# First-batch q in one load per head pair, even tokens above odd ones, and k^T v held in both partition halves

## The chip, the cores and the metric

The kernel runs on one core of one Trainium2 chip. The metric is the device time of one execution in microseconds (us); several executions are timed and their median is told. One further execution is profiled: its instructions, DMA packets and semaphore events are recorded, and "the trace" below means that record.

The core has five engines that run beside one another. TensorE (PE in the profile, with PEld for its weight loads) multiplies matrices from SBUF into PSUM. VectorE (DVE), ScalarE (ACT) and GpSimd (POOL) work on elements. SyncE (SP) here only issues DMA transfers; POOL and ACT issue some as well. They meet through semaphores.

## The reference

```python
# 8 batches, 8 heads, 576 tokens, head_dim 64, all fp32
kv  = einsum('bhsd,bhse->bhde', k, v)            # k^T v, one 64x64 matrix per head, no softmax
out = einsum('bhsd,bhde->bhse', q, kv)           # u = q (k^T v)
out = out / sqrt(mean(out*out, -1) + 1e-6) * g_norm
x   = out.transpose(0, 2, 1, 3).reshape(4608, 512)
gate = sigmoid(x @ w_gate); val = x @ w_val      # 512 -> 1536
return (gate * val) @ w_out                      # 1536 -> 512, float32
```

The three weight matrices arrive as float64 and are converted to fp32 in the kernel.

## The kernel before

**The large part.** The 4608 tokens are worked in 9 chunks of 512 (c = 0 to 8). Chunk 0 uses plain products (lines 666 and 913); the chunks after it use a fast scheme with 26 products instead of 32 or 64 (lines 1037 and 1139), whose sums of operands run on DVE, ACT and POOL beside TensorE. The attention of batch b is worked a stage ahead of the chunks that read it. All of this is behind the change and its instructions are the same before and after, in the same order on TensorE.

**The start, where the change lies.** Before chunk 0 can start, the first batch's eight heads are worked as four pairs, n = 0 to 3, each pair being two neighbouring heads, e = 0 and 1. `load_kv(n)` and `load_q(n)` bring k, v and q of a pair from HBM on SP's queue, in the order k, v, q of pair 0, of pair 1, and so on, with the first unit of weights between. A partition p of the 96 that are used holds six neighbouring tokens, 6p to 6p + 5, of each head (j = 0 to 5). k and v come as one transfer each, in which a partition's piece of one head is a single run of 6 x 64 x 4 = 1536 bytes. q comes as two transfers, one per head, and is laid out as [96, j, e, 64] in SBUF, so each run is 256 bytes.

`attention(n, ...)` returns the steps of a pair, named in the order below by their tokens:

- KV (`kv_mm`, line 346): 12 matmuls of 64 output rows, six tokens j by two heads e. Head e's k^T v lands in PSUM partitions 64e to 64e + 63.
- KVO (`kv_out`, line 350): DVE copies it, [128, 64], to SBUF.
- Q (`q_mm`, line 356): six transposes on TensorE, one per j, of [96, 2 heads x 64] to [128, 96]. So q^T has head 0 in partitions 0 to 63 and head 1 in 64 to 127.
- QO (`q_out`, line 361): ACT copies q^T to SBUF.
- U (`u_mm`, line 373): 20 matmuls of 64 x 64 x 64. The contraction runs over head e's 64 partitions; the result of 64 tokens goes to PSUM partitions r = 0 or 64, alternating, and to PSUM bank e (`ps[:, e]`, 512 fp32 to a bank). The four combinations of the half read (e) and the half written (r) follow one another.
- SQ, SUM, ROOT, NORM (lines 378 to 392): the norm, on ACT and DVE.
- X, XO (lines 400 and 409): five transposes back, and ACT's copies into `xT`, the 512 x tokens operand of the chunks.

The order of everything around these steps is written out by hand in the string `order` (line 699): tokens such as KV0, Q0, KVO0, and between them `warmN` (N matmuls of the identity with itself, whose result nobody reads), `gU.i`/`vU.i` and `agU.i`/`avU.i` (steps of the weights' conversion on DVE and ACT, lines 212 to 254), `bF.i.m` (products of chunk 0, line 666) and `wU` (a load of weights). Each engine runs its own instructions strictly in that order:

```
w1 w2 warm10 KV0 warm4 Q0 KVO0 QO0 warm3 U0 KV1 KVO1 Q1 SQ0 QO1 SUM0 ROOT0 g0.0 warm4 U1 NORM0 SQ1 warm5 X0
SUM1 ag0.0 ROOT1 g0.1 ag0.1 NORM1 XO0 warm1 KV2 Q2 KVO2 QO2 X1 g0.2 XO1 g0.3 warm2 U2 g0.4 v0.0 SQ2 b0.0.0
v0.1 av0.1 SUM2 v0.3 b0.0.1 KV3 ROOT2 av0.0 NORM2 Q3 KVO3 X2 v0.2 w3 g1.0 QO3 U3 XO2 ag1.0 ...
```

In this stage POOL fills the identity and then has nothing to do until it issues the loads of batch 1's q (line 122, from 22 us), which go into memory that the first batch's k, v and q tiles held.

The other attention code, `heads_run` for batches 1 to 7 (line 497), also has 64 x 64 x 64 matmuls, with four combinations of the half read and the half written in turn; its q and k, v come in other layouts, and the change leaves it alone. The tail of k^T v of those batches (line 436) and the rest of it (line 447) are two more kinds of small matmul that are used below: 64 x 64 over two halves read and two halves written, and 128 x 64 over two halves written.

Of the kernel before, what the change touches and what calls it, by code (L numbers as in the profile page):

```python
# [10 lines left out]
FP32 = mybir.dt.float32  # L11
# [10 lines left out]
def kernel(  # L22
# [11 lines left out]
    nc = tc.nc  # L34

    B, H, S, HD = q.shape
    T, DM = out.shape
    DF = moe_w_gate.shape[1]
    P = 128
    NHP = H // 2  # L40
    NJ = 6
    NP = S // NJ
    JH = NJ // 2


    PH = P // 2
    NU = -(-S // P)
# [9 lines left out]
    NRUN = NHP // 2  # L57
    QW = 2 * S

    NK4 = S // P  # L60
    S4 = P * NK4
# [13 lines left out]
    const = ctx.enter_context(tc.tile_pool(name="const", bufs=1))  # L75
# [9 lines left out]
    first = first_ctx.__enter__()  # L85
# [3 lines left out]
    pairs = {n: {} for n in range(B * NHP)}  # L89
# [9 lines left out]

    def load_q(n):  # L100
        h0 = 2 * n
        t = first.tile([NP, NJ, 2, HD], FP32, tag="q", name="q")
        for e in range(2):
            nc.sync.dma_start(out=t[:, :, e, :], in_=q[0, h0 + e].rearrange("(p j) d -> p j d", j=NJ))
        pairs[n]["q"] = t

    q_late = {}
# [190 lines left out]
    for n in range(4):  # L298
        load_kv(n)
        load_q(n)  # L300
        if n in (1, 2):
            load_unit(0, (n - 1,))
# [8 lines left out]
    ident = const.tile([P, P], FP32, name="ident")  # L311


    kvq = const.tile([P, NRUN, 2, HD], FP32, name="kvq")
    kv_ahead = const.tile([P, NRUN, 2, HD], FP32, name="kv_ahead")

    qTs = const.tile([P, QW], FP32, name="qTs")
    sqs = const.tile([P, 2 * NU * P], FP32, name="sqs")
# [13 lines left out]
    def chunk(c):  # L332
        return xT[c]

    def attention(n, at_ps):

        b, m = divmod(n, NHP)
        d = {}
        kv = kvq[:, m // 2, m % 2]

        def kv_mm():
            d["kv"] = ps = at_ps("kv")
            for j in range(NJ):
                js = slice(HD * j, HD * j + HD)
                for e in range(2):
                    nc.tensor.matmul(ps[HD * e:HD * e + HD, 0, 0:HD], pairs[n]["k"][:, e, js], pairs[n]["v"][:, e, js],  # L346
                                     start=(j == 0), stop=(j == NJ - 1))

        def kv_out():
            nc.vector.tensor_copy(out=kv, in_=d["kv"][:, 0, 0:HD])  # L350

        def q_mm():
            d["q"] = ps = at_ps("q")
            for j in range(NJ):
                c0 = NP * (j % JH)
                nc.tensor.transpose(ps[:, j // JH, c0:c0 + NP], pairs[n]["q"][:, j].rearrange("p e d -> p (e d)"),  # L356
                                    ident[0:NP, 0:NP])

        def q_out():
            d["qT"] = qTs[:, S * (n % 2):S * (n % 2) + S]  # L360
            nc.scalar.copy(out=d["qT"].rearrange("p (i n) -> p i n", i=2), in_=d["q"][:, :, 0:JH * NP])  # L361

        def u_mm():


            ps = at_ps("u")
            d["u"] = ps[:, :, 0:NU * HD]
            for i in range(2 * NU):
                t0 = min(PH * i, S - PH)
                r = PH * (i % 2)  # L370
                for e in range(2):
                    es = slice(HD * e, HD * e + HD)
                    nc.tensor.matmul(d["u"][r:r + PH, e, HD * (i // 2):HD * (i // 2) + HD],  # L373
                                     d["qT"][es, t0:t0 + PH], kv[es], start=True, stop=True)

        def u_square():
            d["sq"] = sqs[:, NU * P * (n % 2):NU * P * (n % 2 + 1)].rearrange("p (e c) -> p e c", e=2)
            nc.scalar.activation(out=d["sq"], in_=d["u"], func=AF.Square)

        def u_sum():  # L380
            d["ms"] = sb.tile([P, 2, NU], FP32, tag="ms", name="ms")
            nc.vector.tensor_reduce(out=d["ms"].rearrange("p e i -> p (e i)"),
                                    in_=d["sq"].rearrange("p e (i d) -> p (e i) d", d=HD), axis=AX.X, op=ALU.add)

        def u_root():
            nc.scalar.activation(out=d["ms"], in_=d["ms"], func=AF.Sqrt, bias=eps, scale=1.0 / HD)

        def u_norm():

            nc.vector.reciprocal(d["ms"], d["ms"])  # L390
            d["xn"] = d["sq"].rearrange("p e c -> p (e c)")
            nc.vector.tensor_tensor(out=d["xn"].rearrange("p (i e d) -> p e i d", e=2, d=HD),
                                    in0=d["u"].rearrange("p e (i d) -> p e i d", d=HD),
                                    in1=d["ms"].unsqueeze(3).to_broadcast([P, 2, NU, HD]), op=ALU.mult)

        def x_mm():
            d["x"] = ps = at_ps("x")
            for i in range(NU):
                bank, c0 = divmod(P * i, UX)
                nc.tensor.transpose(ps[:, bank, c0:c0 + P], d["xn"][:, P * i:P * i + P], ident)  # L400

        def x_out():

            s0 = 0
            while s0 < S:
                c, o = divmod(S * b + s0, G)
                i, r = divmod(s0, UX)
                n_ = min(G - o, (UX if i == 0 else S - UX) - r)
                nc.scalar.copy(out=chunk(c)[:, m, o:o + n_], in_=d["x"][:, i, r:r + n_])
                s0 += n_  # L410

        return [kv_mm, kv_out, q_mm, q_out, u_mm, u_square, u_sum, u_root, u_norm, x_mm, x_out]


# [185 lines left out]
    def store(c, t, ot, cols=slice(0, DM), queues=(nc.sync,)):  # L600

        r0 = i = 0
        while r0 < P:
            b, s = divmod(G * c + P * t + r0, S)
            rows = out[S * b:S * b + S, cols]
            if b < NE // NHP:
                j, p = divmod(s, NP)
                n = min(P - r0, NP - p)
                queues[i % len(queues)].dma_start(out=rows.rearrange("(p j) d -> j p d", j=NJ)[j, p:p + n],
                                                  in_=ot[r0:r0 + n, cols])  # L610
            else:

                half, c0 = divmod(s, S // 2)
                n = QB
                queues[i % len(queues)].dma_start(
                    out=rows.rearrange("(p g i) d -> i g p d", p=QB, i=2)[half, c0 // QB],
                    in_=ot[r0:r0 + n, cols])
            r0 += n
            i += 1
# [12 lines left out]
    def mm_ps():  # L632
        return bank((2, 3, 0, 1)[next(turns) % 4])

    def at_ps():
        return psum.tile([P, NAT, 512], FP32, tag="at", name="at")
# [53 lines left out]

    KV, KV_OUT, Q, Q_OUT, U, U_SQUARE, U_SUM, U_ROOT, U_NORM, X, X_OUT = range(11)
    a = [attention(n, early(n)) for n in range(NE)]

    steps = {"KV": KV, "KVO": KV_OUT, "Q": Q, "QO": Q_OUT, "U": U, "SQ": U_SQUARE, "SUM": U_SUM, "ROOT": U_ROOT,
# [13 lines left out]
    for token in order.split():  # L708
        name = token.rstrip("0123456789.")
        n = [int(i) for i in token[len(name):].split(".")]  # L710
# [183 lines left out]
    for some in places.split():  # L894
        p, names = some.split(":")
# [6 lines left out]
    for f in range(2, NFT):  # L902
        if f == NFT - 1:
            last = at_ps()
            ps = last[:, 0], last[:, 1]
        else:
            ps = mm_ps(), mm_ps()
        plain(0, f, ps, {at: at_place.get(2 * NMT * (f - 1) + at, ()) for at in range(2 * NMT)})

    ps = [mm_ps() for _ in range(G // P)]  # L910
# [209 lines left out]
    def second_layer_fast(c, at):  # L1120
# [21 lines left out]
        def finish(i):  # L1142
            _, _, wv, steps = PRODUCTS2[i]
            combine(o, regions, steps, nc.gpsimd)
            give_all(regions, LAST2, i)
            if c > 1 and wv > 7 and wv not in STAY and STREAM.index(wv) + NR < NS:
                load_w((c - 2) * NS + STREAM.index(wv) + NR)
            if c == 1:
                if i in first_loads:
                    load_granule(first_loads[i])  # L1150
            elif i == 16:
                load_granule(NPA * N3 * (c - 1) + NPA - 1)
            if i in dones:
                t = dones[i]
                store(c, t, rows[t], slice(0, DH if c == NG - 1 and t == NT - 1 else DM), ends)
            elif c == NG - 1 and i == 23:
                store(c, NT - 1, rows[NT - 1], slice(DH, DM), ends)
            for step in at.get(next(done), ()):
                step()
            sums_of_h(2)  # L1160
# [38 lines left out]
    for t in range(G // P):  # L1199
        for f in range(NFT - 2, NFT):  # L1200
            second(t, f)
            slot()
        ot = sg_tile()
        nc.scalar.copy(out=ot, in_=ps[t])
        store(0, t, ot)
# [6 lines left out]
    for c in range(1, NG):  # L1212
# [4 lines left out]
        if c + 1 < B:  # L1217
            kv, first_, then = second_batch if c == 1 else feed(c + 1)
# [49 lines left out]
```

## Time and profile before

| | us |
|---|---|
| median of 3 timed executions | 996.3 (996.08 to 996.44) |
| profiled execution | 996.52 |
| its span (first to last instruction of the program) | 994.7 |
| TensorE busy in the span | 989.4 |
| VectorE, ScalarE, GpSimd busy | 715.0, 349.1, 614.1 |
| granted TensorE clock, mean | 1.0 |

The profiled execution spends 1.8 us outside its span. It is 0.2 us longer than the median of the timed ones, so a change of the span in the profile can be added to the median as it is. An fp32 matmul is two records in the trace, a transpose is one. A matmul's record is longer than its share of TensorE's time, since matmuls are pipelined; the time from one record's start to the next one's is what counts for a sum.

### The profile page before, as it was taken

How to read it: one execution, taken by the hardware profiler on the slowest of the kernel's cores; microseconds unless marked ns; L12 is line 12 of the kernel's file. 1: busy time of each engine (PE TensorE's matmuls, PEld its weight loads, DVE VectorE, ACT ScalarE, POOL GpSimd, SP SyncE). 2: the span in 40 equal slices, each digit the busy share in tenths (PEclk: the TensorE clock that was granted, in tenths of full speed). 3: DMA queues.
4: the chain of work that ended last, by engine and by line, in shares of the span. 5: the costliest groups of instructions: out<-in, count | busy, mean ns of one | idle time of the engine just before them, and what ended most of it. 6: DMA issues, size and time to landing. Idle time of an engine off the chain costs nothing.

```text
span 994.7 us, 16605 instructions
## 1 busy us (share of the span) xinstructions
PE 989.4 (99%) x5958; PEld 814.9 (82%) x5958; DVE 715.0 (72%) x1199; ACT 349.1 (35%) x631; POOL 614.1 (62%) x991
## 2 busy tenths in 40 slices
PE   9999999999999999999999999999999999999998
PEld 7454448888888888888888888888888888888887
DVE  5999997898768666785777576866686566756672
ACT  5577523661244213530344124412442133213320
POOL 1349996798169625864386717870786359734963
PEclk9999999999999999999999999999999999999999
DMA  9986507662889568746975677656854455545514
GB/s 275 291 239 219 166 28 210 193 236 89 277 278 282 170 190 275 197 151 195 271 225 162 204 224 248 184 163 210 280 165 156 139 198 190 165 141 172 214 48 123
DMA packets 149523, 194.97 MB, mean 196 GB/s; under 512 B 79840, under 2 KB 121696, under 8 KB 149440
## 3 DMA queue, kind: packets, MB, share of 16 engines
q0 software_dynamic: 22512, 116.41, 35.3%
q1 hardware_dynamic: 120848, 75.66, 26.5%
q10 hardware_dynamic: 6080, 1.84, 0.8%
q8 instruction: 47, 0.77, 0.3%
q14 instruction: 36, 0.29, 0.1%
HBM read 160.04 MB, written 25.56 MB: 187 GB/s over the span
## 4 chain that ended last, share of the span: by engine, by line
PE 99%; ACT 0%; POOL 0%; issue 0%; DVE 0%; POOLq 0%; ACTq 0%
PE mm L1037 54%; PE mm L1139 27%; PE mm L666 7%; PE mm L913 4%; PE at L497 2%; PE mm L727 1%; PE at L447 1%; PE two L666 1%; PE at L666 1%; PE mm L447 1%; PE mm L346 0%; PE two L373 0%; PE two L356 0%; PE at L436 0%; PE two L400 0%; ACT qTs L361 0%
## 5 line engine op out<-in xcount | busy, mean ns | idle before, releaser
L1037 PE MATMUL mm<-xs,w 128*128 128x256 f32 x1428 | 331.3, 379 | 0.0
L1037 PEld LDWEIGHTS mm<-xs,w 128*128 128x128 f32 x1428 | 270.9, 190 | 37.0
L1037 PE MATMUL mm<-xT,w 128*128 128x256 f32 x948 | 230.5, 380 | 0.0
L1037 PEld LDWEIGHTS mm<-xT,w 128*128 128x128 f32 x948 | 179.6, 190 | 25.0 <-issue 0.5
L855 POOL DMA_DIRECT2D w<-kept x84 | 46.9, 559 | 203.1 <-PE mm L1037 199.6
L1007 DVE TENSOR_TENSOR sg<-sg,mm 128x512 f32<-128x512 f32 (+1 forms) x176 | 100.8, 600 | 89.8 <-PE mm L1037 34.3
L1139 PE MATMUL mm<-w,h 128*128 128x256 f32 x630 | 142.9, 379 | 0.0
L1139 PEld LDWEIGHTS mm<-w,h 128*128 128x128 f32 x630 | 119.6, 190 | 16.4 <-POOL h L999 0.2
L1003 ACT COPY temps<-mm 128x512 f32<-128x512 f32 (+1 forms) x128 | 66.0, 537 | 187.1 <-PE mm L1139 94.7
L999 POOL TENSOR_TENSOR h<-h,sg 128x512 f32<-128x512 f32 x72 | 96.6, 1360 | 46.0 <-ACT sg L996 30.2
L808 POOL TENSOR_TENSOR h<-h 128x128 f32<-128x128 f32 x216 | 110.5, 524 | 16.5 <-DVE h_more L808 13.1
L1139 PE MATMUL mm<-w,h_more 128*128 128x256 f32 x474 | 108.2, 379 | 0.0
L996 ACT ACTIVATE sg<-sg 128x512 f32<-128x512 f32 x96 | 59.7, 630 | 127.3 <-DVE sg L1007 127.3
L1139 PEld LDWEIGHTS mm<-w,h_more 128*128 128x128 f32 x474 | 90.1, 190 | 12.2
L1003 ACT COPY sg<-mm 128x512 f32<-128x512 f32 (+1 forms) x112 | 57.1, 510 | 87.5 <-PE mm L1139 45.3
L808 POOL TENSOR_TENSOR h_more<-h 128x128 f32<-128x128 f32 x120 | 58.6, 492 | 34.6 <-DVE h L999 30.3
L1007 DVE TENSOR_TENSOR temps<-temps,mm 128x512 f32<-128x512 f32 (+1 forms) x96 | 59.5, 620 | 26.6 <-PE mm L1139 16.9
L1007 DVE TENSOR_TENSOR temps<-mm,temps 128x512 f32<-128x512 f32 (+1 forms) x64 | 39.9, 623 | 53.3 <-PE mm L1139 23.9
L1003 ACT COPY h<-mm 128x512 f32<-128x512 f32 x48 | 28.1, 585 | 129.9 <-PE mm L1037 116.4
L666 PE MATMUL mm<-xT,w 128*128 128x512 f32 x160 | 70.1, 595 | 0.0
L1007 DVE TENSOR_TENSOR sg<-mm,sg 128x512 f32<-128x512 f32 (+1 forms) x64 | 39.7, 620 | 41.8 <-PE mm L1139 21.9
L808 POOL TENSOR_TENSOR h<-h,h_more 128x128 f32<-128x128 f32 x120 | 60.9, 508 | 4.6
(164 smaller groups left out, 1273.9 us busy)
## 6 DMA issues: line engine op xcount, KB each, us to landing
w<-kept POOLq DMA_DIRECT2D x42, 896.0 KB, 5.4
w<-kept POOLq DMA_DIRECT2D x90, 384.0 KB, 4.3
w<-kept POOLq DMA_DIRECT2D x42, 768.0 KB, 5.0
out_dram<-sg SPq DMA_DIRECT2D x119, 64.0 KB, 1.7
q<-in_q_dram SPq DMA_DIRECT2D x96, 72.0 KB, 5.0
xT<-xTs SPq DMA_DIRECT2D x96, 72.0 KB, 4.4
st<-in_moe_w_gate_dram SPq DMA_DIRECT2D x12, 512.0 KB, 6.2
st<-in_moe_w_val_dram SPq DMA_DIRECT2D x12, 512.0 KB, 6.4
```

The lines of the kernel that those rows point to most:

```text
L447: nc.tensor.matmul(ps[m][HD * g:HD * g + HD, e], mains[2 * m + g, "k"][:, c], mains[2 * m + g, "v"][:, c], start=(b == 2 and e == 0 and j ...
L497: nc.tensor.matmul(to[HD * e:HD * e + HD], qTs[HD * g:HD * g + HD, c:c + HD], kvq[HD * g:HD * g + HD, m, e], start=True, stop=True)
L666: nc.tensor.matmul(self.ps[i], w[("wg", "wv")[i], self.f][:, m, :], xT[self.c][:, m, :], start=(m == 0), stop=(m == NMT - 1), skip_group_c ...
L808: ops.append((eng, lambda v=v, x=x, sign=sign, y=y, eng=eng: eng.tensor_tensor(out=h_form(v, j), in0=h_form(x, j), in1=h_form(y, j), op=op ...
L855: nc.gpsimd.dma_start(out=granule(g)[:, 0:n], in_=kept1[g // NPA % N3, g % NPA][:, 0:n])
L913: nc.tensor.matmul(ps[t], gv[0, f][:, P * t:P * t + P], w["wo", f], start=(f == 0), stop=(f == NFT - 1), skip_group_check=True)
L996: nc.scalar.activation(out=o["o" + step[1]], in_=o["o" + step[1]], func=AF.Sigmoid)
L999: mult.tensor_tensor(out=o[x], in0=o[x], in1=o[y], op=ALU.mult)
L1003: nc.scalar.copy(out=o[out_], in_=o[expr])
L1007: tt(out=o[out_], in0=o[x], in1=o[y], op=ALU.add if sign == "+" else ALU.subtract)
L1037: nc.tensor.matmul(regions[name][1][:, g], ws[:, g], xf[c][wv], start=(new and g == 0), stop=True, skip_group_check=True)
L1139: nc.tensor.matmul(regions[name][1], h_form(hv, j), ws[:, j], start=(used[i] and j == 0), stop=(j == N3 - 1), skip_group_check=True)
```

## The change

Five edits, all in the first batch and in the stores of its result:

- `load_q` brings both heads' q of a pair in one transfer, laid out as [96, e, 6 x 64], so that runs are 1536 bytes like those of k and v. There are four loads in place of eight.
- Each of the six transposes of a pair now takes 128 neighbouring elements of one head: two tokens, 2j and 2j + 1 of the partition's six, by 64. So q^T has even tokens in partitions 0 to 63 and odd ones in 64 to 127, head 0 in the first 288 columns and head 1 in the last.
- So both heads' k^T v are needed in both halves. After DVE's copy of a pair's k^T v, two new copies on GpSimd ([64, 64] each, one from the upper half to the lower, one from the lower to the upper) put the other head's matrix beside it. `kvq` and `kv_ahead` become two parts of one tile, `kvs`, of the same size.
- `u_mm` still has 20 matmuls of 64 x 64 x 64. Half r of the partitions is read and the same half r is written; the bank is still e. The two halves follow one another.
- `x_out` and `store` follow the new order of the tokens.

```diff
     def load_q(n):
         h0 = 2 * n
-        t = first.tile([NP, NJ, 2, HD], FP32, tag="q", name="q")
-        for e in range(2):
-            nc.sync.dma_start(out=t[:, :, e, :], in_=q[0, h0 + e].rearrange("(p j) d -> p j d", j=NJ))
+        t = first.tile([NP, 2, NJ * HD], FP32, tag="q", name="q")
+        nc.sync.dma_start(out=t, in_=q[0, h0:h0 + 2].rearrange("h (p j) d -> p h (j d)", j=NJ))
         pairs[n]["q"] = t
...
-    kvq = const.tile([P, NRUN, 2, HD], FP32, name="kvq")
-    kv_ahead = const.tile([P, NRUN, 2, HD], FP32, name="kv_ahead")
+    kvs = const.tile([P, 2 * NRUN, 2, HD], FP32, name="kvs")
+    kvq, kv_ahead = kvs[:, 0:NRUN], kvs[:, NRUN:2 * NRUN]
...
-        kv = kvq[:, m // 2, m % 2]
+        kv = kvs[:, m]
...
         def kv_out():
-            nc.vector.tensor_copy(out=kv, in_=d["kv"][:, 0, 0:HD])
+            nc.vector.tensor_copy(out=kv[:, 0], in_=d["kv"][:, 0, 0:HD])
+            for r in (0, PH):
+                nc.gpsimd.tensor_copy(out=kv[r:r + PH, 1], in_=kv[PH - r:P - r, 0])

         def q_mm():
             d["q"] = ps = at_ps("q")
-            for j in range(NJ):
-                c0 = NP * (j % JH)
-                nc.tensor.transpose(ps[:, j // JH, c0:c0 + NP], pairs[n]["q"][:, j].rearrange("p e d -> p (e d)"),
-                                    ident[0:NP, 0:NP])
+            for e in range(2):
+                for j in range(JH):
+                    nc.tensor.transpose(ps[:, e, NP * j:NP * j + NP], pairs[n]["q"][:, e, 2 * HD * j:2 * HD * j + 2 * HD],
+                                        ident[0:NP, 0:NP])
...
-            for i in range(2 * NU):
-                t0 = min(PH * i, S - PH)
-                r = PH * (i % 2)
+            for i in range(NU):
                 for e in range(2):
-                    es = slice(HD * e, HD * e + HD)
-                    nc.tensor.matmul(d["u"][r:r + PH, e, HD * (i // 2):HD * (i // 2) + HD],
-                                     d["qT"][es, t0:t0 + PH], kv[es], start=True, stop=True)
+                    t0 = S // 2 * e + min(PH * i, S // 2 - PH)
+                    for r in (0, PH):
+                        nc.tensor.matmul(d["u"][r:r + PH, e, HD * i:HD * i + HD], d["qT"][r:r + PH, t0:t0 + PH],
+                                         kv[r:r + PH, e ^ (r // PH)], start=True, stop=True)
...
-                nc.scalar.copy(out=chunk(c)[:, m, o:o + n_], in_=d["x"][:, i, r:r + n_])
+                src, dst = d["x"][:, i, r:r + n_], chunk(c)[:, m, o:o + n_]
+                if s0 == S4:
+                    src = d["x"][:, i, r:r + P].rearrange("p (g c) -> p g c", g=2)[:, :, PH // 2:PH]
+                    dst = dst.rearrange("p (g c) -> p g c", g=2)
+                nc.scalar.copy(out=dst, in_=src)
...
-                j, p = divmod(s, NP)
-                n = min(P - r0, NP - p)
-                queues[i % len(queues)].dma_start(out=rows.rearrange("(p j) d -> j p d", j=NJ)[j, p:p + n],
+                part, o = divmod(s, P)
+                g, o = divmod(o, PH if part < NK4 else PH // 2)
+                j, p = divmod(PH * part + o, NP)
+                n = min((PH if part < NK4 else PH // 2) - o, NP - p)
+                queues[i % len(queues)].dma_start(out=rows.rearrange("(p j) d -> j p d", j=NJ)[2 * j + g, p:p + n],
                                                   in_=ot[r0:r0 + n, cols])
```

## The prediction

> **What bounds the kernel now.** I read the page first, then TensorE's timeline, then the first 24 us of every engine. The page says that TensorE is the bound, and nearly alone:
>
> ```profile
> PE 989.4 (99%) x5958; PEld 814.9 (82%) x5958; DVE 715.0 (72%) x1199; ACT 349.1 (35%) x631; POOL 614.1 (62%) x991
> PE 99%; ACT 0%; POOL 0%; issue 0%; DVE 0%; POOLq 0%; ACTq 0%
> ```
>
> "Busy" flatters pipelined matmuls, so I also went through the starts of the single matmul records. From 27 us to the last matmul at 990.4 us, every start follows the one before by its kind's usual step, apart from fixed pauses of about 0.1 us on each side of a change between 128-wide and 64-wide matmuls, and one pause of 0.04 us at 224.6. So after the start nothing waits that TensorE could make up: a microsecond that the change puts on TensorE in the start is a microsecond at the end, and one that it takes from another engine counts only where TensorE waits for it. The chain of waits in the first 24 us shows where that is:
>
> ```profile
> 8.26 0.70 PE mm L727 x6
> 8.99 0.81 PE two L373 x40
> 9.80 0.85 PE mm L346 x24
> 10.65 0.65 PE two L356 x6
> 11.29 0.92 PE mm L727 x8
> 12.21 0.74 PE two L373 x40
> ...
> 21.11 0.66 PE two L356 x6
> 21.84 0.65 ACT qTs L361
> 22.50 0.04 issue
> 22.54 0.81 PE two L373 x40
> ```
>
> Columns: start, length, what. The links are TensorE's own work, with the dummy products of L727 between; only before U3 does ACT's copy of q^T stand in the chain. No DMA stands in it. The landings against their first use say the same: k0 and v0 land at 3.77 and 4.82 us and are used at 5.75; q0 6.90, 7.49; v1 9.37, 9.73; q2 15.21, 15.81; v3 19.54, 20.18; q3 20.62, 21.04. The real waits of TensorE up to 27 us, beyond the fixed pauses, are about 0.10 us (U0, for ACT), 0.08 (the first chunk product at 18.27, for DVE's weight), 0.07 (X2) and 0.12 (U3, for ACT): 0.4 us in all.
>
> **Part 1, the q loads: 0.** SP issues four transfers fewer, of 0.57 to 0.74 us of issue each. 4608 packets of 256 bytes, 18 ns each in the trace, become 768 of 1536 bytes, 65 to 101 ns (medians of k's and v's): 83 us become about 65 on 16 DMA engines, so some 1.1 us of DMA time less by 20 us, and weights that land up to that much earlier. TensorE waits for no landing, so this is worth nothing; at most it takes the 0.08 us of DVE's wait for the first weight (landed 11.70, used 11.73) and a part of the 0.4 above.
>
> **Part 2, Q, QO, X, XO: 0.** The same six transposes of [96, 128], the same copy of 576 columns, the same five transposes back; XO's last copy reads two pieces of 32 columns in place of 64 in one. One store more, at the end of chunk 0, on SP beside 99% TensorE.
>
> **Part 3, U: +2.33 us.** The count of matmuls stays at 20 per pair, 40 records. What changes is which quarter of the array each uses. Before, the four combinations of half read and half written follow one another; after, only (lower, lower) and (upper, upper) occur. What that costs is seen from how TensorE packs small matmuls:
>
> ```profile
> 55.27 0.27 PE L436 MATMUL at<-h_more 64*64 64x64 f32 x2
> 55.28 0.27 PE L436 MATMUL mm<-h_more 64*64 64x64 f32 x2
> 55.38 0.22 PE L436 MATMUL at<-h_more 64*64 64x64 f32 x2
> 55.39 0.23 PE L436 MATMUL mm<-h_more 64*64 64x64 f32 x2
> 55.44 0.23 PE L436 MATMUL at<-h_more 64*64 64x64 f32 x2
> 55.45 0.23 PE L436 MATMUL mm<-h_more 64*64 64x64 f32 x2
> ```
>
> The first column is the start. L436 issues, per head, two matmuls into `at` (rows 0 to 63 of the operands, the two output halves) and two into `mm` (rows 64 to 127). Each is two records, yet the records start as one of each of the four, then, 58 ns later, the next of each: four quarters at a time, and a quarter's own records one after another. U before does the same: its records start in fours (9.093, 9.099, 9.106, 9.113; then 9.151, 9.158 ...), ten steps of 58 ns. KV has two column halves, and its records start in twos at the same 58 ns, twelve steps for 24 records. The chain agrees: 0.85 us for KV's twelve steps, 0.74 for U's ten.
>
> After the change U has two quarters in use, so twos: 20 steps in place of 10. Ten steps of 58.3 ns are +0.58 us per pair, and four pairs +2.33 us. All of it is on TensorE, in a stretch where it hardly waits. It absorbs the 0.08 us before 18.27, since by then TensorE is 1.7 us later and DVE's weight at most 1.2 (only U0 and U1 are ahead of it). The waits of X2 and U3 stay, since NORM2 and QO3 hang on TensorE's own shifted work. So +2.25 us.
>
> A rule of the Trainium skill speaks against this layout. TensorEngine Tiling (Array Packing), Restrictions and Gotchas, "PSUM Pressure", says that different row tiles go to different PSUM banks and cannot use one bank at the same time. By it the two quarters of the new U, which read different halves and write one bank, would not overlap at all. No row of before shows that case, and the first rival below prices it.
>
> **Part 4, GpSimd's copies: 0, or up to +1.6.** The second matmul of each U now waits for the second copy. The trace has no such copy. Rows around it:
>
> ```profile
> 0.74 0.20 POOL masks.py:197 MEMSET ident<- 128x128 f32 x1 [0.29 <-POOLq L1252]
> 1.02 0.29 POOL masks.py:199 TENSOR_SCALAR_AFFINE_SELECT ident<-ident 128x128 f32<-128x128 f32 x1
> L808 POOL TENSOR_TENSOR h_more<-h 128x128 f32<-128x128 f32 x120 | 58.6, 492 | 34.6 <-DVE h L999 30.3
> ...
> 21.52 0.21 DVE L350 COPY kvq<-mm 128x64 f32<-128x64 f32 x1
> 22.06 5.65 POOL L122 DMA_DIRECT2D h<-in_q_dram  x8 [20.75 <-DMA st<-in_moe_w_val_dram]
> ```
>
> L808's two-input add takes 0.44 us at best for 128 columns and L826's 0.72 for 256, so 0.30 for 64 by their line; a copy has one input less, and the shortest POOL row, a memset of one column, is 0.09. So a copy is between 0.1 and 0.3 us, two in series 0.2 to 0.6, plus 0.08 from DVE to POOL and 0.05 from POOL to TensorE (both seen elsewhere in the trace). From the end of KVO to the start of U there are 2.05 us for pair 0, 1.22 for pairs 1 and 2, 0.81 for pair 3 (21.73 to 22.54), and KVO and U shift together. Even 0.73 us fits each time. The bound above: beside DVE's conversions L826's adds have taken up to 1.79 us against 0.72, 2.5 times. Two copies at 0.75 are then late by 0.4 for U1 and U2 and 0.8 for U3, together 1.6 us. The bound below is 0, since a wait cannot gain. I take 0, by the rows nearest in size. Behind the copies POOL has the loads of L122. They start some 2 us later; their data land by 33 and 41 us and DVE turns them from 46.4 on, which covers it. Behind the waiting matmul stands all of TensorE, so a late copy counts in full.
>
> **The sum.** 0 + 0 + 2.33 - 0.08 + 0 = +2.25 us: span 994.7 to 997.0, profiled execution 996.5 to 998.8. It stands 0.2 above the median, so the median goes from 996.3 to about 998.5, +0.23%. What a measurement here can tell from no change is 0.2%, 2.0 us; the forecast lies close above that.
>
> **The rivals.**
>
> *One bank, no overlap.* If the two quarters cannot write one bank together, each U takes 40 steps in place of 10: 30 x 58.3 ns = 1.75 us per pair, +7.0, so 1003.2 us. For it: wherever the kernel has two halves read at once (L436, L497, U before) they write different banks. Against: two halves written share a bank freely in KV and L447, where the partitions differ, as they do here; what would clash is the same partitions. Chance 0.09.
>
> *Late copies.* GpSimd's two copies take the place of QO as what U waits for. It decides from 0.34 us a copy for U3, from 0.55 for U1 and U2. For it: DVE is busy without a break from 16 to 18.5 us and after 20.5, much of it two-input work, and adds on POOL have been stretched beside such work; KVO3 has the shortest window. Price 0.1 to 1.6 us on top: 998.6 to 1000.2, at 1 us a copy 1001.7. Chance 0.10.
>
> *Not slower.* U's ten more steps do not show: the records of one quarter would have to overlap. Then only the gain of part 1 and the copies are left, 995.9 to 996.5 us. With half of the steps it would be 997.4. It decides where a pair's U grows by less than 0.5 us. For it: in U before, the two records of a matmul are never alone in a step, so what a quarter by itself can do is not shown. Against: L727 and L666 have one quarter's worth, the whole array, and never start two records together; KV starts two, not four. Chance 0.10.
>
> *Faster.* All real waits of TensorE in the start are 0.4 us, so even all of them are within the 0.2%. It would need something that the profile does not show. Chance 0.03.
>
> **How the numbers follow.** The forecast, two records a step and the copies hidden, has 0.68. Its time is 998.5, and since the bound for "slower" is 998.3, I count 0.12 of it as within 0.2%. Slower: 0.56 + 0.09 + 0.10 = 0.75. Same: 0.12 + 0.10 = 0.22. Faster: 0.03. The range goes down to 997.4 (half of the steps) and up to 1001.2 (nearly all of the late copies); it leaves out the one-bank case, the whole of "not slower" and "faster", about 2 in 10.
>
> **What would show it.** In the new profile, U's four rows in the chain should grow from about 0.74 to 1.32 us at 40 records each, their records starting in twos every 58 ns; KV, Q and X should keep their lengths; the first long run of L666 (36.5 us before) should start 2.2 to 2.3 us later, and the last matmul too. GpSimd should show eight copies of at most 0.3 us that end before ACT's qTs copy. U at 2.5 us says one bank; a pause between U's first and second matmul says late copies; U unchanged says that the packing is not what I read. A last matmul that moves by something else than the start did would prove the first step wrong, that TensorE's stream behind 27 us has no slack.

## The result, and the profile after

The change makes the kernel slower. Six executions each: 996.46 us before (996.08 to 996.84), 1000.29 after (999.78 to 1000.76); ratio 1.0039, 95% interval 1.0026 to 1.0051. That is +3.8 us where +2.25 was forecast. In the profiles the span goes from 994.7 to 998.0 us, +3.28. Of that, +2.63 is there when the last matmul starts (990.44 to 993.07), and +0.64 comes after it.

The page of after: busy time by engine, then the shares of the chain that ended last.

```profile
PE 991.6 (99%) x5958; PEld 817.9 (82%) x5958; DVE 715.4 (72%) x1199; ACT 348.8 (35%) x631; POOL 615.3 (62%) x999
PE 97%; DMA 2%; SPq 0%; ACT 0%; issue 0%; DVE 0%; ACTq 0%
```

TensorE is still the bound, but 2% of the chain, some 20 us, are now DMA. The chain counts a transfer from its issue to its landing; TensorE's own waits for q are much shorter (below). The chain in the first 27 us (start, length, what) shows which transfers they are:

```profile
3.26 7.64 DMA q<-in_q_dram
10.89 0.02 issue
10.91 12.33 DMA q<-in_q_dram
23.24 0.14 issue
23.38 0.70 PE two L357 x6
```

Q3 (L357) starts when q3 lands, and SP had issued q3 only when q1 had landed: SP's and ACT's transfers take eight semaphores in turn, and a transfer is issued only when the one that had its semaphore has landed (q1 lands at 10.89, q3 is issued at 10.91). Before, no transfer stood in this chain. The landings, before and after: v0 4.82 and 5.42 us, q0 6.90 and 7.53, q1 9.93 and 10.89, q2 15.21 and 17.24, q3 20.62 and 23.24. The same bytes in fewer, longer packets arrive later.

U in the timeline of after (start, length, engine, line, shapes, records; in brackets the idle time before it and what ended it):

```profile
9.30 1.38 PE L373 MATMUL two<-kvs,qTs 64*64 64x64 f32 x40
13.03 1.38 PE L373 MATMUL two<-kvs,qTs 64*64 64x64 f32 x40
18.99 1.44 PE L373 MATMUL two<-kvs,qTs 64*64 64x64 f32 x40
24.84 1.52 PE L373 MATMUL two<-kvs,qTs 64*64 64x64 f32 x40 [0.22 <-ACT qTs L362]
```

The same view of before:

```profile
8.99 0.81 PE L373 MATMUL two<-kvq,qTs 64*64 64x64 f32 x40
12.14 0.81 PE L373 MATMUL two<-kvq,qTs 64*64 64x64 f32 x40
17.45 0.81 PE L373 MATMUL two<-kvq,qTs 64*64 64x64 f32 x40
22.54 0.81 PE L373 MATMUL two<-kvq,qTs 64*64 64x64 f32 x40
```

The records of after start in twos 58 ns apart, so U0 and U1 are 0.57 longer. U2 and U3 are longer still, by 0.06 and 0.14: their second matmul waits for GpSimd. GpSimd's eight copies (least, middle and longest time in ns, first and last start):

```profile
L351 POOL COPY kvs<-kvs x8: 231/284/632, 7.4 to 24.6; 64x64 f32<-64x64 f32 x8
```

And the waits of TensorE in the first 36 us of after (total us, times, longest), neither of which stood in the same view of before:

```profile
PE two L373 <- ACT qTs L362: 0.2, 1, 0.2
PE two L357 <- DMA q<-in_q_dram: 0.2, 1, 0.2
```

Comparing the starts of the 5958 matmul records one by one, after against before, gives the account of the two profiles:

| term | predicted, us | profiles, us |
|---|---|---|
| up to the end of KV0: TensorE goes to full speed later in this run | - | +0.32 |
| U, 20 steps instead of 10, four pairs | +2.33 | +2.28 |
| U2 and U3 wait for GpSimd's copies | 0 | +0.21 |
| late q: Q2 +0.08, Q3 +0.22, U3's start +0.16, X2's own wait -0.16 | 0 | +0.30 |
| waits absorbed: before 18.27, -0.08; in 26 to 31 us, -0.32; rest, -0.07 | -0.08 | -0.47 |
| from the last matmul's start to the end of the span, 4.30 to 4.94 | 0 | +0.64 |
| sum | +2.25 | +3.28 |

### The profile page after: what moved, and what is told of

Its sections match the earlier page's. It is cut to its first block, busy times and chain, and to the rows that moved or that the text cites. A ratio compares the mean times of both kernels' runs of the same rounds, so it can differ in the third digit from the quotient of the medians.

```text
span 998.0 us, 16615 instructions
## 1 busy us (share of the span) xinstructions
PE 991.6 (99%) x5958; PEld 817.9 (82%) x5958; DVE 715.4 (72%) x1199; ACT 348.8 (35%) x631; POOL 615.3 (62%) x999
## 4 chain that ended last, share of the span: by engine, by line
PE 97%; DMA 2%; SPq 0%; ACT 0%; issue 0%; DVE 0%; ACTq 0%
PE mm L1043 54%; PE mm L1145 27%; PE mm L672 7%; PE mm L919 4%; DMA q<-in_q_dram 2%; PE at L501 2%; PE at L451 1%; PE two L672 1%; PE at L672 1%; PE mm L451 1%; PE at L440 0%; SPq L97 0%; PE two L373 0%; PE two L357 0%; ACT qTs L362 0%
```

## The experiments

Each was timed in five rounds with runs of the kernel before on the same chip; ratios are to those. A ratio of 1.001 is 1.0 us. The theory after the result, theory A in the expectations: U's steps cost what was forecast; the long runs of q delay the landings, and these are a second bound behind U, hidden in after by U's own length; GpSimd's copies and the end add the rest. The rival is the forecast's own: only U's steps count.

**U alone.**

```diff
-  d["u"][r:r + PH, e, HD * (i // 2):HD * (i // 2) + HD], ...
+  d["u"][HD * e:HD * e + HD, r // PH, HD * (i // 2):HD * (i // 2) + HD], ...    # in before
```

> The kernel before with only U's placing changed: head e's matmuls write half e of the partitions and the bank of the parity of i, so only (lower, lower) and (upper, upper) occur, as after; loads, copies and the rest are those of before (the output is permuted). Prediction's part 3: 20 steps of 58.3 ns instead of 10, U +0.58 us in each pair, +2.2 to +2.4 us at the last matmul and in the time. Rival, the two quarters cost nothing by themselves and the loss comes from loads and copies: 0 to 0.3. Rival, two row halves in one bank don't overlap: +7.

Ratio 1.0012 (1.0003 to 1.0021); span 997.3. In its chain U0 and U3 read:

```profile
9.81 1.38 PE two L373 x40
...
25.00 1.37 PE two L373 x40
```

Against the control's profile (below), each U is 0.57 longer, 2.3 in sum, and the last matmul 1.72 later: 0.40 is absorbed between 26 and 32 us and 0.3 is a pause that the control has in KV2 and this kernel has not. So U's growth is the steps of its two quarters, with nothing of loads and copies in it. The time pays a part of it: +1.2 us (0.3 to 2.1), under the +2.2 to +2.4 that was expected. The one-bank rival (+7) is refuted: two quarters that read different halves and write different halves of one bank overlap in full. By the Trainium skill, TensorEngine Tiling (Array Packing), "PSUM Pressure", they could not use one bank at a time; here the trace disagrees, with starts in twos 58 ns apart.

**The load alone.**

```diff
-        for e in range(2):
-            nc.sync.dma_start(out=t[:, :, e, :], in_=q[0, h0 + e].rearrange("(p j) d -> p j d", j=NJ))
+        nc.sync.dma_start(out=t.rearrange("p (h a) e d -> p h (a e d)", h=2),
+                          in_=q[0, h0:h0 + 2].rearrange("h (p j) d -> p h (j d)", j=NJ))    # in before
```

> The kernel before with one change: a pair's q comes in one transfer of 1536-byte runs (into the same tile and read by the same transposes, so that q's tokens and heads are permuted). Theory A, from the landings in the trace after (q2 17.24 us against 15.21, q3 23.24 against 20.62): the longer runs land later, and with U still short TensorE reaches Q2 at about 16.0 and Q3 at about 21.2, so it waits 1.2 to 2.0 us for q: +1.5 to +2.2 us against before, with a wait for DMA q ahead of Q2 or Q3. Rival, the prediction's part 1: no landing is waited for, 0 (within 0.3 us).

> e1_load_alone again, for a second profile. In the first, 1.69 us of the loss was a pause of TensorE inside KV2 that waits for no semaphore (16.39 to 18.30 us); the control has a shorter one, 0.27, at the same place. If that pause is a chance of one run, the profile here has a wait for DMA q ahead of Q2 or Q3 instead, of 0.3 to 1.2 us, or none; the timed median tells what the load alone costs: +1.5 to +2.5 again if it is lasting, +0.4 to +0.8 (the end alone) if not.

Ratio 1.0020 (1.0011 to 1.0029), and again 1.0020 (1.0012 to 1.0029): the load, forecast at 0, costs some 2 us by itself. But theory A had the wrong place for it. The chain of the second profile around KV2 (L346), and the waits of TensorE up to 36 us:

```profile
15.60 0.78 PE mm L346 x21
16.39 1.05 issue
17.44 0.33 PE mm L346 x3
```

```profile
PE mm L346 <- issue: 1.1, 1, 1.1
PE two L356 <- DMA q<-in_q_dram: 0.6, 2, 0.4
```

TensorE stops in the middle of KV2, with its operands there, and waits for no semaphore: 1.1 us here and 1.7 in the first profile, at the same place, after 21 of KV2's 24 records. The two waits for q are ahead of Q0 and Q1, not Q2 and Q3. The longer end makes +0.40 in both profiles (4.70 us after the last matmul's start, against 4.30).

What KV2 may wait for can be looked for in the DMA records. Every profile has one packet of 16384 bytes on an instruction queue that ends between 13.6 and 16.7 us; in the first of these two runs (DMA queues from 12 to 20 us: packets, MB, share):

```profile
q8 instruction: 1, 0.02, 1.0%
```

It ends at 16.73 us there and TensorE goes on at 18.30; in the second run 15.82 and 17.44; in the control 15.00 and 16.50. In all three TensorE resumes 1.50 to 1.62 us after the fetch. A fourth profile, that of "nobody waits for the copies" below, has a pause of 0.07 us at the same place, which ends 1.53 us after the fetch. The other ten reach the record 1.4 us or more after the fetch and don't stop: 13.59 and 15.60 in before, 15.50 and 17.06 in after. One of them fits less well: before with seven transfers more passes the record 1.40 us after the fetch, sooner than any that stopped went on. The fetch ends at 13.6 to 15.1 us in the seven profiles with 256-byte runs of q, and at 15.3 to 16.7 in the six with one long transfer. So the fetch lands later with the long transfer. If the pauses are waits for it, the longer runs delay TensorE's next instructions too, and after is spared because its slower U brings it to that record 1.56 us after the fetch. By the Trainium skill, Runtime: NRT & Kernel Launch, "Instruction fetch mechanics", engines refill their instruction memory in blocks of 16 KiB by a DMA queue of their own, at a cost that is mostly hidden; the packet's size agrees, and if the pauses are this fetch, it was not hidden here. That the packet is TensorE's is inferred from the coincidences in time; no run took the fetch away.

**The short runs back, in after.**

```diff
-        nc.sync.dma_start(out=t, in_=q[0, h0:h0 + 2].rearrange("h (p j) d -> p h (j d)", j=NJ))
+        for e in range(2):
+            nc.sync.dma_start(out=t.rearrange("p h (a c d) -> p (h a) c d", a=3, c=2)[:, :, e],
+                              in_=q[0, h0 + e].rearrange("(p j) d -> p j d", j=NJ))
```

> The kernel after with the loads of before: two transfers of 256-byte runs for a pair's q, into the tile and for the transposes of after (q's tokens and heads are permuted). Theory A: q2 and q3 land at 15.2 and 20.6 us as before, the waits ahead of KV0, Q2 and Q3 (0.17, 0.10, 0.25 us) go, and U's 2.3 and some 0.1 to 0.2 for GpSimd's copies are left: +2.2 to +2.6 us against before at the last matmul, 0.3 to 1.0 us under after. Rival, the prediction's part 1: the load is worth nothing, the time is that of after, +3.3 to +3.8.

Ratio 1.0023 (1.0014 to 1.0032), where theory A has +2.2 to +2.6 at the last matmul; after itself has 1.0039, and two variants of it, further on, 1.0033 and 1.0036. The intervals overlap, so the time alone doesn't settle it, and the trace agrees in part. q2 lands at 14.24 us, q3 at 21.33, nothing waits for DMA. But the last matmul starts 3.02 us after that of before, and 2.63 in after. Of the 3.02, 0.70 is there by the end of KV0 (late full speed); without that it is 2.3, as in after. What the landings gave, GpSimd's copies took: 0.15 in U2 and 0.36 in U3, more than in after, since U3 no longer comes late for q's sake. Only the end is shorter, 4.47 us against 4.94. So the 1.6 us between the two ratios are not explained by this profile.

How busy the DMA engines are early separates the profiles with short runs from those with one long transfer. The window from 4 to 5.5 us (busy time of each engine, clock, DMA share, GB/s), of before and then of after:

```profile
4.00:5.50 1.50, 1.50 (x9) 1.50 (x8) 0.00 (x0) 0.00 (x0) 0.00 (x0) 1.00 0.98 238
```

```profile
4.00:5.50 1.50, 1.50 (x9) 1.50 (x8) 0.00 (x0) 0.00 (x0) 0.00 (x0) 1.00 0.55 152
```

Share 0.94 to 1.04 and 221 to 246 GB/s in the seven profiles with short runs, 0.54 to 0.65 and 125 to 152 in the six with one long transfer, though six transfers are issued by 3.7 us and not all have landed. Why the engines idle then stays open. The later landings follow with a spread from run to run: q2 lands at 14.24 to 16.27 us in the seven and at 15.97 to 17.81 in the six, q3 at 20.47 to 21.97 and at 21.57 to 24.23; on average 1.8 and 1.7 us later with the long transfer.

**Two long transfers.**

```diff
+        for e in range(2):
+            nc.sync.dma_start(out=t[:, e], in_=q[0, h0 + e].rearrange("(p j) d -> p (j d)", j=NJ))    # in after
```

> The kernel after with a pair's q in two transfers, one per head, each of 1536-byte runs; the result is complete. It tells the length of the runs from the size and number of the transfers. If the length of the runs delays the landings: DMA share at 4 to 6 us about 0.3 to 0.7 as after, q2 at about 17 us, time as after, +3 to +3.8. If it is the fewer and larger transfers: DMA share near 1.0 at 4 to 6 us as before, q2 at about 15 us, +2.2 to +2.8 us as with the short runs.

Ratio 1.0028 (1.0017 to 1.0039): it fits both. So does the trace. The share from 4 to 5.5 us is 0.70 (179 GB/s), nearer the long transfers; q0 and q1 land at 7.18 and 10.57, as with short runs (at most 7.25 and 10.73; with one long transfer at least 7.53 and 10.85); q2 lands at 16.07, where the two groups overlap. So the length of the runs was not told apart from the number and size of the transfers.

**U in four quarters, in after.**

```diff
-  nc.tensor.matmul(d["u"][r:r + PH, e, HD * i:HD * i + HD], ...
+  nc.tensor.matmul(d["u"][PH * e:PH * e + PH, r // PH, HD * i:HD * i + HD], ...
```

> The kernel after, with U's results put so that all four combinations of half read and half written follow one another (half of the partitions written = head, PSUM bank = half read; the tokens of two halves change places, so the output is permuted). Steps of U: 10 of 58 ns instead of 20, U 0.8 us instead of 1.4. If U's steps are the whole, the time is 2.3 us under after, +1.0 to +1.5 against before. If the long load's late landings are a second bound behind U (theory A), only part of it comes back: Q2 and Q3 then wait for q at 17.3 and 23.3 us, and the time is about that of the long load alone, +1.5 to +2.3 against before.

Ratio 1.0020 (1.0011 to 1.0029), though each U is back at 0.81: the second bound, as theory A has it. TensorE's waits up to 36 us name it, though not where it was expected: KV2 and KV3 wait 1.1 and 1.0 us for v, and less is waited for q:

```profile
PE mm L345 <- DMA v<-in_v_dram: 2.1, 2, 1.1
PE two L357 <- DMA q<-in_q_dram: 0.6, 3, 0.3
```

**Both undone** (the last two edits together).

> Both undone at once: the kernel after with U in four quarters (as e3_four_quarters) and q in two transfers of 256-byte runs (as e2_after_short_runs); GpSimd's copies, the transposes of neighbouring tokens and the store order of after stay (output permuted). Theory A (U's steps and late landings are two bounds that cover each other): -0.3 to +0.6 us against before; KV2, KV3, Q2, Q3 wait for no landing, and what is left is U3's wait for GpSimd, 0.1 to 0.3. Rival, something else in the change (the store, the copies, the transposes) costs 1 us or more: +1.2 to +2 against before.

Ratio 1.0009 (1.0000 to 1.0018): +0.9, a little over the +0.6 that theory A allowed. No wait for a landing is left. The last matmul starts 0.90 after that of the first profile of before, of which 0.81 is there by the end of KV0 (TensorE's late full speed) and 0.5 is GpSimd's copies (U2 +0.16, U3 +0.38), less 0.45 absorbed as before. The end is 5.00 us instead of 4.30. So what is left of the change when U and the load are undone is mostly the end.

Whether the two bounds cover each other on average stays open. In the times they add up: +1.2 us for U alone, +2.0 for the load alone, +3.3 to +3.9 for both (after and two variants of it), and in after the undoing of the load brings 1.6, that of U 1.9 and that of both 3.0, though the intervals of neighbours overlap. In the profiles they cover each other: counted from the end of KV0, so without the late full speed, the last matmul starts later than in before by 1.8 us with U alone, by 1.9 and 2.2 with the load alone, and by 2.3 in after.

**Nobody waits for the copies.**

```diff
-                                         kv[r:r + PH, e ^ (r // PH)], start=True, stop=True)
+                                         kv[r:r + PH, 0], start=True, stop=True)    # in after
```

> The kernel after, where U's second half reads DVE's own copy of k^T v (so each second half multiplies with the other head's matrix), and nobody waits for GpSimd's two copies, which are still made. Theory: the copies hold up U2 and U3 by 0.1 to 0.3 us in sum; the time is 0 to 0.4 under after, +2.9 to +3.6 against before. Rival, late copies are the unexplained part of the loss: 0.8 to 1.5 under after.

Ratio 1.0033 (1.0021 to 1.0045), about 0.6 us under after and inside its interval. U2 and U3 in its timeline:

```profile
19.46 1.38 PE L373 MATMUL two<-kvs,qTs 64*64 64x64 f32 x40
25.03 1.38 PE L373 MATMUL two<-kvs,qTs 64*64 64x64 f32 x40
```

1.38 against 1.44 and 1.52: by the trace the copies are 0.2 us of after, not the missing 1.5. The time alone can't tell. The last matmul starts no earlier than in after (993.16 us, against 993.07), since Q0 waited 0.5 us for q0 in this run.

**The control.**

> The kernel before itself, as a control: ratio 1.000 within 0.0005. In its profile I look at three things that changed between runs of the same loads: when TensorE's 128-wide products go from steps of 0.21 to 0.11 us (5.5 us in the first profile of before, 6.1 to 7.3 in the others; if that is a matter of the run, it falls anywhere from 5.4 to 7.4 here), when q2 and q3 land (15.2 and 20.6 in the first, 16.3 and 22.0 in e7_before_two_quarters with the same loads), and the time after the last matmul (4.3 us in the first).

Ratio 1.0001 (0.9993 to 1.0010). Its span is 995.6, 0.9 over the first profile of the same kernel, and all of that arises in the start: KV0 ran at half speed (5.93 us to 7.24 instead of 5.75 to 6.60), and KV2 paused at the place described above (0.33 us later at Q2).

```profile
5.93 1.37 PE L346 MATMUL mm<-v,k 96*64 96x64 f32 x24
```

Its end is 4.29 us.

**The end: is it the turn of the semaphores?** One store of chunk 2 is cut into more transfers, 2 in after and 8 in before:

```diff
+                parts = 2 if (c, t, r0) == (2, 0, 0) else 1
+                for k in range(parts):
+                    k0, k1 = n * k // parts, n * (k + 1) // parts
...
```

> The kernel before with seven transfers more: the same store of chunk 2 cut in eight, so that the last stores take the semaphores that they have in after. If the turn of the semaphores sets the end: 4.9 to 5.2 us after the start of the last matmul instead of 4.29, and +0.6 to +0.9 us. If not: 4.3 us and no difference. The start is that of before in either case.

> The kernel after with one transfer more: one store of chunk 2 (32 rows) is cut in two, at about 355 us, where SP has time. After has three stores more and four loads fewer than before, one transfer fewer in all on the eight semaphores that SP's and ACT's transfers take in turn; with one more, the last stores take the same semaphores as in before. If the longer end (4.94 us after the last matmul starts, against 4.30) comes from that turn: 4.3 us again, and the time 0.6 us under after, +2.6 to +3.1 against before. If it comes from anything else in the change: 4.9 to 5.2.

DVE's last instruction in the timeline of after, and then of before with seven transfers more, under the view's first line with the span:

```profile
core 0 of [0], span 998.0 us
...
993.49 0.42 DVE L1013 TENSOR_TENSOR sg<-mm,temps 128x256 f32<-128x256 f32 x1 [0.88 <-PE mm L1145]
```

```profile
core 0 of [0], span 995.6 us
...
990.86 0.42 DVE L1010 TENSOR_TENSOR sg<-mm,temps 128x256 f32<-128x256 f32 x1 [0.87 <-PE mm L1142]
```

The program ends 4.1 and 4.3 us after that last addition; in before, 3.46 us (990.85 + 0.42 to 994.73):

```profile
990.85 0.42 DVE L1007 TENSOR_TENSOR sg<-mm,temps 128x256 f32<-128x256 f32 x1 [0.87 <-PE mm L1139]
```

Seven transfers more, 640 us earlier, made the end of before 5.12 us instead of 4.30, with the last matmul at 990.44 as ever; ratio 1.0005 (0.9996 to 1.0013), within the noise of the time. So transfers far ahead do change the end. That the turn alone sets it is not shown. After with one transfer more has the turn of before and an end of 4.55, about halfway back; its ratio of 1.0036 (1.0022 to 1.0050) can't show it. The three profiles with the turn and the stores of before have 4.27 to 4.30, the four with after's turn 4.94 to 5.17. But three kernels that share a third turn (short runs back, two long transfers, both undone) have 4.47, 4.61 and 5.00.

The semaphores' updates in the traces split the end in two. The last store lands 3.08 to 3.11 us after the last matmul's start in the five profiles with before's number of stores, whatever their turn, and 3.27 to 4.02 in the nine with more stores. From there to the end it is 1.15 to 1.28 us with before's turn, 0.97 to 0.98 with the third, and 1.57 to 1.59 with after's, where SP's closing waits, taken in a fixed order, have a pause of 0.4 us that no landing explains; with seven transfers more it is 1.21. So of after's 0.64 us, 0.24 is the later landing and 0.40 the closing waits, which go with the turn, while the seven transfers moved the landing alone, by 0.80. Why the stores land later, and why the turn matters, stays open.

**All three undone** (both undone, with the store cut in six).

> e4_quarters_short_runs with its end mended as well: five transfers more by the same cut, eight more than before in all, so the last stores take the semaphores of before. The kernel after, then, but for the four quarters (output permuted), the 256-byte runs and the turn of the semaphores; GpSimd's copies and the transposes stay. If these three are the whole loss: within 0.3 us of before and 4.3 us after the last matmul's start. If the copies or the transposes cost something by themselves, +0.5 or more.

Ratio 1.0004 (0.9995 to 1.0013): not to be told from before, as expected; with up to 1.3 us in the interval, the time doesn't exclude 0.5 for the copies. In the trace they hold up U2 by 0.16 and U3 by 0.38, most of which later waits take back by 31 us. The end is 4.54, again about halfway, and its profile has 0.4 us at 712 us that no other has.

## Why the prediction was right, and what it missed

Slower was right, and the time lies inside the range. TensorE's steps are the largest term of the two profiles, 2.28 of 3.28 us; by the times alone they can't be told from the load (+1.2 for U alone, +2.0 for the load alone, with overlapping intervals). That the time lies inside is in part luck: the range reached to 1001.2 for the sake of late copies, which cost 0.2 us, and most of what came on top of the forecast came from terms that it had at 0. By the steps:

- **Part 3, U:** right in mechanism and size. U's four blocks grew by 0.57 us each, 2.28 for 2.33, in twos every 58 ns; alone in before it makes the same growth. The absorbed 0.08 before 18.27 came as said, but 0.32 to 0.40 more is absorbed behind it (next point).
- **"From 27 us to the last matmul no slack":** not quite. The steps from 26.4, 26.9 and 30.0 us were 0.10, 0.08 and 0.14 us longer than usual in before, on no change between 128-wide and 64-wide matmuls. They are gone in after, so they were waits, and gave back 0.32 us. Up to the end of U3 the start moved by 3.02 us, the last matmul by 2.63.
- **Part 1, the loads, 0:** this step failed. "TensorE waits for no landing" was read correctly from before, but the margins (0.6 us for q2, 0.4 for q3) were held against a landing that could only come earlier. I priced packets by their own time and took the sum as the time of the transfer. Those times were not fixed: in before the 1536-byte packets of k and v took 85 ns on average, in after all those of q, k and v 99, so that the packet times of the three add up to 228 us instead of 219, and not to 18 less (209 to 228 in the six profiles with one long transfer, 214 to 232 in the seven with short runs). The first weight lands at 12.92 instead of 11.70, not earlier, and q up to 2.6 us later in after. The load alone costs some 2 us; beside the slower U it is 0.3 in the profile of after, where U's 2.3 us of delay cover the later landings; the times do not show that cover.
- **Part 4, the copies, 0:** the term was too small, inside its bounds. A copy takes 0.23 us in pairs 0 and 1 and 0.33 to 0.63 in pairs 2 and 3, beside DVE's conversions, not 0.1 to 0.3; U2 and U3 wait 0.2 us in sum. "Late copies" is the rival that came true in part.
- **Part 2, the store, 0:** the extra stores cost nothing in their place, but the end is 0.64 us longer. The number of transfers ahead has to do with it; how is open. No step of the forecast looked at what follows the last matmul.
- **Not slower, faster, one bank:** refuted; U grew by the full 0.57 in every pair, and not by 1.75.

The forecast is 1.8 us under the measured median. The profiles account for 1.0 of that: +0.64 from the end, +0.30 from the landings, +0.21 from the copies and +0.32 from the late full speed, less 0.39 of absorbed waits and 0.05 from U. Of the rest, 0.5 is that the profiled execution of after, 999.78 us, is the fastest of its six, and 0.2 that before has 996.46 here instead of 996.3.

## What to carry to other kernels

A layout that left one diagonal of TensorE's quarters unused made U's 64 x 64 products take 1.38 us instead of 0.81, and this could be read beforehand from the starts of other small matmuls. A wait that does not exist is worth nothing, but a load with a margin of half a microsecond can become a bound as soon as it moves, so price a changed load by both signs. Where two bounds may cover each other, undo them one by one and together, and compare the timed medians as well as the profiles: here the two did not agree.

## What the runs showed of the hardware that was not expected

- **Full speed comes at a different time in each run.** TensorE's 128-wide products start at 1.36 us in every profile in steps of 0.21 us; the steps become 0.11 at 4.5 us in three profiles, 5.5 to 5.8 in three, 6.3 in two and 7.0 to 7.5 in six, whatever the kernel. It moves the end of KV0 by up to 1.3 us, of which later waits take back a part. The granted clock reads 1.00 all the while. The Trainium skill, TensorE: Matmul & The Clock Gate, Part 1, has a free-running window of about 3.4 us and a transition around 4 us into sustained matmul work, give or take 0.5. The trace agrees with a change of factor two that depends on the run, and shows a wider spread: 3.1 to 6.1 us after the first product.
- **Shorter packets filled the DMA engines sooner.** 256-byte runs of q kept them at a share of 0.94 to 1.04 at 4 to 5.5 us, 1536-byte runs at 0.54 to 0.65 in one transfer and 0.70 in two.
- **TensorE stopped in the middle of a run of matmuls with its operands there,** for 0.3, 1.1 and 1.7 us, and went on 1.5 to 1.6 us after a 16384-byte fetch on an instruction queue had ended. That it waited for its own instructions is inferred.
- **The time after the last matmul, 4.3 to 5.2 us,** changed with transfers far ahead: seven more, 640 us earlier, made it 5.12 us instead of 4.30 (one profile).
